# Plain 32-bit products for the first 16 slots of a fused attention and MLP kernel, with a lead of one slot and a new order of the lead-in

## The chip, the cores and the metric

The kernel runs on one core of one Trainium2 chip. The metric is the device time of one launch in microseconds, as the median of several runs.

## What is computed

Batch 8, 8 heads, 576 tokens, head dimension 64; 32 packed queries per head. Attention goes in two steps, then come two MLPs one behind the other, on 4608 tokens:

```python
p_packed = sm_attn(p, k, v)
out = sm_attn(q, p_packed, p_packed)
x = out.transpose(0, 2, 1, 3).reshape(4608, 512)
h = np.maximum(x @ w_in, 0.0)
x = h * h @ w_out
h = x @ w_in2
return (h * (1.0 / (1.0 + np.exp(-1.702 * h)))) @ w_out2
```

The four weights arrive as 64-bit floats and are turned into 32-bit ones on the chip. `w_in` and `w_in2` are 512 x 2048, the other two 2048 x 512.

## The kernel before, in words

**Slots.** The first MLP is cut into slots, one for each (batch b, half hf of 288 tokens, block fc of 128 hidden units). `runs` (L645) lists their order: slots 0 to 3 are (0, 0, fc 0 to 3), 4 to 11 are (0, 1, fc 0 to 7), 12 to 15 are (0, 0, fc 4 to 7), 16 to 31 are the two halves of batch 1 with fc 0 to 7, 32 to 63 are fc 8 to 15 of both batches. From slot 64 on each half takes its 16 blocks in one go. The attention's last product is folded into the MLP: `m_step` (L363) multiplies the packed values by `w_in` into M, and `mm1` (L377) multiplies M by the attention weights `a`. `mm1` is followed by a ReLU and a square on ScalarE, `gsplit` (L393) splits the result, and `mm2` (L397) multiplies by `w_out` into four PSUM banks. In mm1 two inner blocks, in mm2 four output blocks make the products of a slot.

**Split products.** An operand is split into a rounded high part (a copy on ScalarE into the type fp32r) and the rest (a subtraction on VectorE); a product is then three matmuls of fp32r, high by high, high by low, low by high (`prod`, L80). mm1 is 6 and mm2 12 matmuls of 288 columns. The products of the attention itself, `heads` (L247), are plain 32-bit floats; in the trace each of them is two instructions.

**Lead.** The loop at L888 emits, for slot s, `gsplit` of slot s + LA - 1, `mm1` of slot s + LA and `mm2` of slot s, with LA = 3, and then the steps planned for slot s. Each engine runs its instructions in the order in which they are emitted. Steps that are generators are interleaved with each other at their yields (`interleave`, L687).

**Conversions.** A weight block of 128 x 512 is loaded raw (`raw_load`, four buffers), turned into two 32-bit parts on ScalarE (`conv_a`, L113) and joined in three instructions on VectorE (`conv_b`, L122). A block of `w_out` is then split as well (`wo_item`, L143). The list `cq` (L657) is their order; a step `convert` does part b of one item, part a of the next, and `ahead` then issues the raw load of a later one on SP, which waits until a raw buffer is free. `win_item` (L201) also stores pairs of converted blocks of `w_in` to DRAM (`win_d`), from where the later batches load them.

**Lead-in.** Slots -10 to -1 hold the attention of batch 0: `s1` (scores), `s1b` (exponentials), `tr` (transposes), `pv`, `t2`, then `s2a`, `s2b`, `s2c` for each half of the queries, `m_step`, and transposes of the identity called `warm` (L697). The table `first` (L713) is written by hand and also holds the steps of batch 1's attention and the conversions up to slot 35. The loads of batch 1 stand at L764 to L787: keys and values in slot -4, queries in slots 0 to 4, `w_in` from slot 5 on. SP issues all transfers from one queue, in order.

**Rest.** From slot 256 on the second MLP runs in another scheme (L806 on), which the change does not touch.

Of the kernel before, what the change touches and what calls it, by code (L numbers as in the profile page):

```python
# [44 lines left out]
def fused_kernel(ctx, tc, qT, kT, vv, pT, w_in, w_out, w_in2, w_out2, out):  # L45
# [155 lines left out]
    def win_item(f, c):  # L201
        g = c // 2

        def dst():
# [4 lines left out]
        def done(x):
            if c % 2:  # L210
                nc.sync.dma_start(out=win_d[:, f, 2 * g:2 * g + 2, :], in_=wt[0, f, g])

        return conv_item(f"win{f}_{c}", w_in[c * P:(c + 1) * P, f * 512:(f + 1) * 512], dst, done)
# [183 lines left out]
    def mm2(b, hf, fc, seg):  # L397

        t = gh.pop((b, hf, fc))
        w = wo1[fc // 4]  # L400

        ops = [(d, w_, 0) for d in range(NDM) for w_ in (0, 1)] + [(d, 0, 1) for d in range(NDM)]
        for d, w_, x_ in ops:
            if fc == seg[0] and (w_, x_) == (0, 0):
# [522 lines left out]
```

## Time and profile before

| | |
|---|---|
| three runs | 1450.52, 1443.46, 1443.74 us; median 1443.74 |
| the profiled execution | 1446.43 us |
| its span in the profile | 1444.6 us |
| TensorE busy (page, part 1) | 1417.5 us, 98% |
| VectorE, ScalarE busy | 955.2 us (66%), 837.3 us (58%) |
| mean granted clock | 0.993 |

A span is shown from its own start. PE is TensorE, DVE VectorE, ACT ScalarE, SPq the queue of SyncE that issues transfers; a row of a timeline is start, length, engine, line, operation, written tile <- read tiles, count, and in brackets the idle time before it with what ended it.

### The profile page before, as it was taken

Reading aid. Unit: us, or ns where it says so; the run is one execution under the profiler, and the core shown is the slowest. Engines: PE = TensorE matmul, PEld = TensorE weight load, DVE = VectorE, ACT = ScalarE, POOL = GpSimd, SP = SyncE. Lnnn points to the kernel's source line nnn. Section 1 sums busy time; section 2 is a strip of 40 time slices with the busy share of each in tenths; the row PEclk is TensorE's granted clock in tenths of the full one; section 3 lists DMA queues with packets and bytes.
Section 4 is the critical chain, followed back from the end, with each engine's and each line's share of the span. In section 5 each row is a group of like instructions: output and inputs, shape, how many; then the busy total and the mean of one; then the engine's idle time right before and its main releaser. Section 6 shows DMA issues by size and latency. Waiting matters only on the chain.

```text
span 1444.6 us, 24988 instructions
## 1 busy us (share of the span) xinstructions
PE 1417.5 (98%) x9786; PEld 1268.4 (88%) x9786; DVE 955.2 (66%) x1633; ACT 837.3 (58%) x1748; POOL 0.7 (0%) x6
## 2 busy tenths in 40 slices
PE   6799999999999999999999999999999999999999
PEld 4679989989999898999998888888888889999998
DVE  5787476665757748563255778568756876677585
ACT  3888667667676767766564544455444634544452
POOL 0000000000000000000000000000000000000000
PEclk8899999999999999999999999999999999999999
DMA  8756657586574765642145567656765676688675
GB/s 303 241 191 217 227 179 251 164 260 204 184 238 152 257 207 182 201 155 77 50 159 173 205 226 251 217 183 245 252 218 184 217 250 235 251 305 290 253 294 179
DMA packets 110934, 307.95 MB, mean 213 GB/s; under 512 B 9056, under 2 KB 52192, under 8 KB 96736
## 3 DMA queue, kind: packets, MB, share of 16 engines
q1 hardware_dynamic: 110816, 306.35, 61.9%
q8 instruction: 77, 1.26, 0.4%
q14 instruction: 41, 0.34, 0.1%
HBM read 250.94 MB, written 55.38 MB: 212 GB/s over the span
## 4 chain that ended last, share of the span: by engine, by line
PE 90%; DMA 3%; DVE 3%; ACT 3%; issue 1%; SPq 0%; ACTq 0%; DVEq 0%
PE h L86 36%; PE y L406 25%; PE o L86 24%; PE m L255 2%; DMA w_d<-wc 1%; PE s L255 1%; PE pv L313 1%; PE tr_a L301 1%; DMA wA<-w_d 1%; DMA win<-win_d 0%; DMA k<-in_kT 0%; ACT M L370 0%; ACT gh L77 0%; ACT r L385 0%; ACT gf L390 0%
## 5 line engine op out<-in xcount | busy, mean ns | idle before, releaser
L406 PE MATMUL y<-gh,wo 128*128 128x288 f32 x3072 | 449.6, 295 | 3.3 <-ACT ysb L419 2.5
L406 PEld LDWEIGHTS y<-gh,wo 128*128 128x128 f32 x3072 | 421.0, 189 | 4.7 <-ACT ysb L419 3.5
L86 PE MATMUL h<-y,wA 128*128 128x512 f32 (+1 forms) x1680 | 349.5, 367 | 0.2 <-DMA wA<-w_d 0.2
L86 PE MATMUL o<-g,wB 128*128 128x512 f32 (+1 forms) x1680 | 348.9, 367 | 0.0
L86 PEld LDWEIGHTS h<-y,wA 128*128 128x128 f32 x1680 | 305.6, 188 | 40.6 <-issue 0.5
L86 PEld LDWEIGHTS o<-g,wB 128*128 128x128 f32 x1680 | 305.7, 188 | 39.3 <-DMA wB<-w_d 0.2
L86 PE MATMUL h<-a,M 128*128 128x288 f32 x1536 | 257.6, 303 | 8.4 <-ACT a L359 3.0
L86 PEld LDWEIGHTS h<-a,M 128*128 128x128 f32 x1536 | 217.7, 190 | 52.7 <-issue 29.1
L517 ACT ACTIVATE g<-hid 128x1024 fp32r<-128x1024 f32 (+1 forms) x140 | 132.8, 971 | 131.9 <-DVE hid L512 105.3
L78 DVE TENSOR_TENSOR gh<-gf,gh 128x288 fp32r<-128x288 f32 x256 | 115.6, 453 | 123.7 <-ACT gh L77 123.4
L493 DVE TENSOR_TENSOR g<-hid,g 128x1024 fp32r<-128x1024 f32 (+1 forms) x140 | 152.7, 1115 | 42.5 <-ACT g L517 41.2
L385 ACT ACTIVATE r<-h 128x288 f32<-128x288 f32 x256 | 104.0, 406 | 86.5 <-PE h L86 85.9
L581 ACT ACTIVATE r<-h 128x512 f32<-128x512 f32 (+1 forms) x120 | 66.5, 554 | 117.1 <-PE h L86 115.0
L589 DVE TENSOR_TENSOR hid<-h,r 128x512 f32<-128x512 f32 (+1 forms) x120 | 76.2, 635 | 80.2 <-PE h L86 64.3
L77 ACT ACTIVATE gh<-gf 128x288 fp32r<-128x288 f32 x256 | 112.0, 438 | 4.5 <-DVE gf L388 2.7
L599 DVE TENSOR_TENSOR hid<-hid,sg 128x512 f32<-128x512 f32 (+1 forms) x120 | 76.0, 634 | 47.2 <-ACT sg L595 47.2
L390 ACT ACTIVATE gf<-r 128x288 f32<-128x288 f32 x220 | 97.9, 445 | 7.0
L595 ACT ACTIVATE sg<-hid 128x512 f32<-128x512 f32 (+1 forms) x120 | 70.2, 585 | 30.6 <-DVE hid L589 30.3
L372 DVE TENSOR_TENSOR M<-m,M 128x512 fp32r<-128x512 f32 x64 | 43.3, 689 | 46.0 <-ACT M L370 45.2
L512 DVE TENSOR_TENSOR hid<-hid 128x1024 f32<-128x1024 f32 (+1 forms) x60 | 66.1, 1112 | 0.0
L370 ACT ACTIVATE M<-m 128x512 fp32r<-128x512 f32 x64 | 37.1, 595 | 43.6 <-PE m L255 43.5
L255 PE MATMUL m<-win,ppT 64*32 64x512 f32 x512 | 37.7, 615 | 5.8 <-DVE s2t L334 5.0
(93 smaller groups left out, 916.7 us busy)
## 6 DMA issues: line engine op xcount, KB each, us to landing
wB<-w_d SPq DMA_DIRECT2D x70, 1024.0 KB, 4.9
wA<-w_d SPq DMA_DIRECT2D x40, 1024.0 KB, 4.9
wA<-w_d SPq DMA_DIRECT2D x40, 768.0 KB, 6.1
win<-win_d SPq DMA_DIRECT2D x56, 512.0 KB, 5.3
w_d<-wc SPq DMA_DIRECT2D x112, 256.0 KB, 4.0
k<-in_kT SPq DMA_DIRECT2D x32, 288.0 KB, 5.4
y_d<-ysb SPq DMA_DIRECT2D x16, 576.0 KB, 3.8
v<-in_vv SPq DMA_DIRECT2D x16, 512.0 KB, 6.9
```

Source lines behind the costliest of these rows:

```text
L77: nc.scalar.activation(hi, src, AF.Copy)
L78: nc.vector.tensor_tensor(out=lo, in0=src, in1=hi.bitcast(F32), op=ALU.subtract)
L86: nc.tensor.matmul(ps, w, x, start=start and i == 0, stop=stop and i == n - 1, skip_group_check=more)
L255: nc.tensor.matmul(ps[r][32 * hp:32 * hp + 32, :n], w(hp)[rows], xx, start=True, stop=True)
L385: nc.scalar.activation(r, ps[:, :HS], AF.Relu)
L390: nc.scalar.activation(g, r, AF.Square)
L406: nc.tensor.matmul(accs[d][:, :HS], w[:, fc % 4, w_, d * P:(d + 1) * P], t[:, x_, :], start=fc == seg[0] and (w_, x_) == (0, 0), stop=fc = ...
L493: nc.vector.tensor_tensor(out=t[:, :, 1, :n], in0=src, in1=t[:, :, 0, :n].bitcast(F32), op=ALU.subtract)
L517: nc.scalar.activation(t[:, :, 0, :PAIRS[p]], gop[p, i, g, "src"], AF.Copy)
L589: nc.vector.tensor_tensor(out=hid(p, c, blk), in0=bank[p, c, b][:, :n], in1=part[p, c, r][:, 0, :n], op=ALU.add)
L595: nc.scalar.activation(t, bank[p, c, "1"][:, :n] if blk == 2 else hid(p, c, blk), AF.Sigmoid, scale=GELU)
L599: nc.vector.tensor_tensor(out=hid(p, c, blk), in0=bank[p, c, "1"][:, :n] if blk == 2 else hid(p, c, blk), in1=part.pop((p, c, "sg", blk)), ...
```

## The change

The products of the slots of batch 0 with fc below 8 (16 slots, NFULL = 8) are made in plain 32-bit floats, without splits: `mm1` is two products, `mm2` four. M for these blocks is copied by ScalarE alone; M and `a` share a tile (`mf_tile`), the converted blocks 0 to 7 of `w_out` lie unsplit in one tile. The splits of those blocks (`wo_split`) and of `a` (`a_split`) are made later, in slots 10 to 19, 23 and 28, for the slots that use them. The lead is one slot up to slot 7, two up to slot 10 and three after. Slots -10 to -2 become one list, `lead_in`, in which each step is run to its end before the next (`drain`). Conversions 0 to 15 are steps `ca` and `cb` with fixed places; the list `cq` has another order; the stores of `w_in` become steps of their own (`win_store`); batch 1's loads move to slots 0, 1 and 3 to 7. Some steps use other PSUM banks, and for batch 0 the copies of `tr` change engines.

```diff
+NFULL = 8
+NDIR = 16
...
+        def dst():
+            if fc == 0:
+                wo1["f"] = wo_p.tile([P, NFULL, DM], F32, tag="wo", name="wof")
+            return wo1["f"][:, fc]
+
         def use(x):
-            if fc % 4 == 0:
-                wo1[fc // 4] = wo_p.tile([P, 4, 2, DM], F32R, tag="wo", name=f"wo{fc // 4}")
-            w = wo1[fc // 4][:, fc % 4]
-            nc.scalar.activation(w[:, 0, :], x, AF.Copy)
-            yield
-            nc.vector.tensor_tensor(out=w[:, 1, :], in0=x, in1=w[:, 0, :].bitcast(F32), op=ALU.subtract)
-
-        return conv_item(f"wo{fc}", w_out[fc * P:(fc + 1) * P, :], use=use)
+            return wo_split(fc, x)
+
+        return conv_item(f"wo{fc}", w_out[fc * P:(fc + 1) * P, :], *((dst,) if fc < NFULL else (None,)),
+                         use=no_use if fc < NFULL else use)
+
+    def wo_split(fc, x=None):
+        if fc % 4 == 0:
+            wo1[fc // 4] = wo_p.tile([P, 4, 2, DM], F32R, tag="wo", name=f"wo{fc // 4}")
+        w = wo1[fc // 4][:, fc % 4]
+        return late_split(w[:, 0, :], w[:, 1, :], wo1["f"][:, fc] if x is None else x)
+
+    def late_split(hi, lo, x):
+
+        nc.scalar.activation(hi, x, AF.Copy)
+        yield
+        nc.vector.tensor_tensor(out=lo, in0=x, in1=hi.bitcast(F32), op=ALU.subtract)
...
+    def win_store(f):
+        for g in range(2):
+            nc.sync.dma_start(out=win_d[:, f, 2 * g:2 * g + 2, :], in_=wt[0, f, g])
...
+        ta_ = t[:, 0:4, :].rearrange("p c k -> p (c k)")
+        if b == 0:
+            nc.vector.tensor_copy(ta_, pa_)
+            nc.scalar.activation(t[:64, 4, :], pb_[:64, :P], AF.Copy)
+        else:
+            nc.scalar.activation(ta_, pa_, AF.Copy)
+            nc.vector.tensor_copy(t[:64, 4, :], pb_[:64, :P])
...
+    def s2p(b, hf):
...
+    def a_split(hf):
+        a = a_tile(0, hf)
+        return late_split(a[:, :, 0, :], a[:, :, 1, :], mf_tile(hf)[:, 1024:1024 + S].rearrange("p (u n) -> p u n", u=2))
...
+        if b == 0 and 4 * f < NFULL:
+            for r in range(2):
+                nc.scalar.activation(mf_tile(f)[:, 512 * r:512 * r + 512], ps[r], AF.Copy)
+            return
...
+        if full(b, fc):
+            for g in range(2):
...
+                nc.tensor.matmul(ps[:, :HS], w, mf_tile(hf)[:, 1024 + g * HS:1024 + (g + 1) * HS], start=g == 0, stop=g == 1)
...
+            t = gh[b, hf, fc] = gh_p.tile([P, 2, HS], F32, tag="gh", name=f"gh_{b}_{hf}_{fc}")
+            nc.scalar.activation(t[:, 0, :], r, AF.Square)
...
+            ops = [(d, 0, wo1["f"][:, fc]) for d in range(NDM)]
...
+    for w in ((0, 0), (0, 1), (0, 2), (0, 3), range(0, 4), (1, 0), (1, 1), (1, 2), (1, 3), range(4, 12), (2, 0), (2, 1), (2, 2), (2, 3),
+              (3, 0), (3, 1), (3, 2), (3, 3), range(12, 16)):
...
+    for f, *a in ((load_p, 0), (load_k, 0, 0), (load_k, 0, 1), (load_k, 0, 2), (load_k, 0, 3), (ahead,), (ahead,),
+                  (load_v, 0, 0), (load_v, 0, 1), (ahead,), (load_q, 0, 0, 0), (load_q, 0, 1, 0),
+                  (load_q, 0, 2, 0), (load_q, 0, 3, 0), (ahead,)):
         at(S0, f, *a)
 
+    lead_in = [(s1, 0, 0), (s1, 0, 1), (warm, 14), (ca, 0), (s1b, 0), (cb, 0), (tr, 0, 0), (ca, 1), (tr, 0, 1), (cb, 1),
+               (warm, 8), (ca, 2), (pv, 0, 0), (pv, 0, 1), (warm, 2), (t2, 0), (load_q, 0, 0, 1), (load_q, 0, 1, 1),
+               (load_q, 0, 2, 1), (load_q, 0, 3, 1), (cb, 2), (ca, 3), (s2p, 0, 0), (warm, 24),
+               (s2a, 0, 0), (ca, 4), (cb, 3), (win_store, 0), (m_step, 0, 0), (s2b, 0, 0), (ca, 5), (s2p, 0, 1), (warm, 6)]
+    for f, *a in lead_in:
+        at(S0, drain, f, *a)
+    nconv = 6
...
-        -10: [(warm, 14), (s1, 0, 0), (s1, 0, 1)],
...
+        -1: [(cb, 4)],
+        0: [(cb, 5), (ca, 6)],
+        1: [(s2a, 0, 1), (cb, 6), (ca, 7)],
+        2: [(s2b, 0, 1), (cb, 7), (ca, 8), (s1, 1, 0)],
+        3: [(s1, 1, 1), (cb, 8), (ca, 9), (cb, 9), (ca, 10)],
+        4: [(cb, 10), (s1b, 1), (ca, 11), (cb, 11)],
+        5: [(win_store, 1), (m_step, 0, 1), (ca, 12), (cb, 12)],
+        6: [(tr, 1, 0), (ca, 13), (cb, 13), (ca, 14)],
+        7: [(pv, 1, 0), (tr, 1, 1), (cb, 14), (ca, 15)],
+        8: [(pv, 1, 1), (t2, 1), (cb, 15)],
+        9: [(s2a, 1, 0)],
+        10: [(s2b, 1, 0), (wo_split, 0), (wo_split, 1)],
+        11: [(s2c, 1, 0), (m_step, 1, 0), (convert,)],
+        12: [(wo_split, 2), (convert,)],
+        13: [(wo_split, 3), (convert,)],
+        14: [(s2a, 1, 1)],
         15: [(m_step, 1, 1)],
-        16: [(convert,)],
-        17: [(convert,)],
-        18: [(s2b, 1, 1)],
-        19: [(s2c, 1, 1), (convert,)],
-        21: [(m_step, 0, 2)],
-        23: [(convert,)],
-        24: [(convert,)],
+        16: [(wo_split, 4), (convert,)],
+        17: [(wo_split, 5), (convert,)],
+        18: [(s2b, 1, 1), (wo_split, 6)],
+        19: [(s2c, 1, 1), (wo_split, 7)],
...
+        23: [(a_split, 0), (convert,)],
+        24: [(win_store, 2), (m_step, 0, 2), (convert,)],
...
+        28: [(a_split, 1), (convert,)],
...
-            at_k, at_v, at_q, at_w = -4, -4, (0, 2, 3, 4), 5
+            at_k, at_v, at_q, at_w = 0, 1, (3, 5, 6, 7), 7
...
+    nsplit = nfirst = 0
     for s in range(S0, len(slots)):
-        if 0 <= s + LA - 1 < len(slots):
-            slots[s + LA - 1][1](*slots[s + LA - 1][3])
-        if 0 <= s + LA < len(slots):
-            slots[s + LA][0](*slots[s + LA][3])
+        la = LA if s > 10 else 2 if s > 7 else 1
+        while nsplit < min(s + la, len(slots)):
+            slots[nsplit][1](*slots[nsplit][3])
+            nsplit += 1
+        while nfirst < min(s + la + 1, len(slots)):
+            slots[nfirst][0](*slots[nfirst][3])
+            nfirst += 1
```

## Rows read from the trace of the kernel before

**Rows 1.** The page, part 4: the chain that ended last, by engine.
```profile
PE 90%; DMA 3%; DVE 3%; ACT 3%; issue 1%; SPq 0%; ACTq 0%; DVEq 0%
```

**Rows 2.** Busy time by stretch: us, each engine (instructions), PEclk, DMA share, GB/s.
```profile
0.00:107.77 107.77, 85.93 (x765) 66.25 (x766) 79.12 (x164) 74.49 (x166) 0.70 (x6) 0.90 0.72 245
103.00:143.00 40.00, 39.31 (x319) 36.34 (x318) 33.12 (x65) 33.48 (x77) 0.00 (x0) 1.00 0.61 203
```

**Rows 3.** Timeline of TensorE, 0 to 175 us.
```profile
18.83 2.95 PE L702 MATMUL warm<-ident 128*128 128x128 f32 x14
...
23.16 1.75 PE L702 MATMUL warm<-ident 128*128 128x128 f32 x14
...
46.30 0.46 PE L86 MATMUL h<-a,M 128*128 128x288 f32 x1 [2.96 <-ACT a L359]
...
72.49 0.90 PE L313 MATMUL pv<-v,e1t 128*32 128x64 f32 x40
73.32 0.66 PE L301 MATMUL tr_a<-ident,e 128*128 128x128 f32 x4
...
80.34 0.71 PE L255 MATMUL s<-q,ppT 64*32 64x288 f32 x16
...
107.77 0.95 PE L86 MATMUL h<-a,M 128*128 128x288 f32 x6
108.55 1.75 PE L406 MATMUL y<-gh,wo 128*128 128x288 f32 x12
110.14 0.95 PE L86 MATMUL h<-a,M 128*128 128x288 f32 x6
...
119.72 1.09 PE L255 MATMUL m<-win,ppT 64*32 64x512 f32 x16
```

**Rows 4.** Groups by form on TensorE: count, busy us, mean ns, idle before.
```profile
L255 PE MATMUL m<-win,ppT 64*32 64x512 f32 x512 | 37.7, 615 | 5.8 <-DVE s2t L334 5.0 <-DMA win<-win_d 0.8
L255 PE MATMUL s<-k,p 64*32 64x288 f32 x256 | 13.8, 421 | 1.8 <-DMA k<-in_kT 1.2 <-ACT e L269 0.6
```

**Rows 5.** The chain in order of time, 0 to 140 us: start, length, what.
```profile
10.61 2.04 ACT e L284 x8
...
13.21 0.57 ACT r_win L120
```

**Rows 6.** Timeline of VectorE, 0 to 62 us.
```profile
13.49 0.41 DVE L124 TENSOR_SCALAR win<-win 128x512 int32<-128x512 int32 x1
...
14.77 0.69 DVE L128 SCALAR_TENSOR_TENSOR win<-raw_win,win 128x512 int32<-128x512 int32 x1
...
19.01 0.48 DVE L334 STREAM_TRANSPOSE s2t<-s 128x288 f32<-128x288 f32 x1 [0.95 <-PE s L255]
...
23.55 0.75 DVE L336 TENSOR_REDUCE s2st<-s2t 128x18 f32<-128x576 f32 x1
...
28.40 0.78 DVE L354 STREAM_TRANSPOSE s2x<-s2t 128x576 f32<-128x576 f32 x1
```

**Rows 7.** Timeline of ScalarE, 0 to 62 us.
```profile
25.60 0.68 ACT L343 ACTIVATE s2t<-s2t 128x576 f32<-128x576 f32 x1 [1.62 <-DVE s2t L338]
...
32.93 1.08 ACT L370 ACTIVATE M<-m 128x512 fp32r<-128x512 f32 x2 [3.04 <-PE m L255]
...
37.60 0.61 ACT L148 ACTIVATE wo<-x_wo 128x512 fp32r<-128x512 f32 x1
```

**Rows 8.** Busy time by stretch of 2 us, columns as in rows 2.
```profile
20.00:22.00 2.00, 2.00 (x10) 1.56 (x9) 0.96 (x3) 1.25 (x2) 0.00 (x0) 0.50 1.02 414
24.00:26.00 2.00, 0.91 (x9) 0.67 (x7) 1.56 (x3) 0.40 (x1) 0.00 (x0) 1.00 0.16 66
46.00:48.00 2.00, 1.37 (x5) 1.10 (x6) 1.93 (x4) 2.00 (x5) 0.00 (x0) 0.62 0.35 139
48.00:50.00 2.00, 2.00 (x10) 2.00 (x10) 1.97 (x6) 1.97 (x5) 0.00 (x0) 0.52 0.01 2
```

**Rows 9.** The page, part 6: transfers: count, KB each, us from issue to landing.
```profile
k<-in_kT SPq DMA_DIRECT2D x32, 288.0 KB, 5.4
```

More of the change, by code (lines that the diff above doesn't have):

```diff
@@ L207, in dst @@
             return wt[0, f, g][:, c % 2, :]
[L209 to L213, printed above, removed]
+        return conv_item(f"win{f}_{c}", w_in[c * P:(c + 1) * P, f * 512:(f + 1) * 512], dst)
+    def win_store(f):
+        for g in range(2):
+            nc.sync.dma_start(out=win_d[:, f, 2 * g:2 * g + 2, :], in_=wt[0, f, g])
     kt, qt, vt, pt, wt = {}, {}, {}, {}, {}
@@ L326, in fused_kernel @@
     NB = HS // 32
+    def s2p(b, hf):
+        ps = s2t[b, hf] = [att_tile(b, hf == 0, f"s2_{b}_{hf}_{r}") for r in range(2)]
+        heads(ps, lambda hp: ppT[b][:, 32 * hp:32 * hp + 32], lambda hp: qt[b, hp][:, hf * HS:(hf + 1) * HS])
     def s2a(b, hf):
-        ps = [att_tile(b, False, f"s2_{b}_{hf}_{r}") for r in range(2)]
-        heads(ps, lambda hp: ppT[b][:, 32 * hp:32 * hp + 32], lambda hp: qt[b, hp][:, hf * HS:(hf + 1) * HS])
+        if (b, hf) not in s2t:
+            s2p(b, hf)
+        ps = s2t[b, hf]
         t = s2_p.tile([P, 2 * NB, 32], F32, tag="s2t", name=f"s2t{b}_{hf}", bufs=1)
@@ L375, in fused_kernel, with full @@
     gf, gh, ys = {}, {}, {}
+    def full(b, fc):
+        return b == 0 and fc < NFULL
     def mm1(b, hf, fc, seg):
@@ L399, in mm2 @@
         t = gh.pop((b, hf, fc))
[L400 to L404, printed above, removed]
+        if full(b, fc):
+            ops = [(d, 0, wo1["f"][:, fc]) for d in range(NDM)]
+        else:
+            w = wo1[fc // 4][:, fc % 4]
+            ops = [(d, 0, w[:, i]) for d in range(NDM) for i in (0, 1)] + [(d, 1, w[:, 0]) for d in range(NDM)]
+        for n, (d, x_, w) in enumerate(ops):
+            first = fc == seg[0] and d not in {o[0] for o in ops[:n]}
+            if first:
                 accs[d] = acc_p.tile([P, 512], F32, tag=f"acc{d}", name=f"y_{b}_{hf}_{d}_{fc}")
-            nc.tensor.matmul(accs[d][:, :HS], w[:, fc % 4, w_, d * P:(d + 1) * P], t[:, x_, :],
-                             start=fc == seg[0] and (w_, x_) == (0, 0), stop=fc == seg[1] and x_ == 1)
+            nc.tensor.matmul(accs[d][:, :HS], w[:, d * P:(d + 1) * P], t[:, x_, :],
+                             start=first, stop=fc == seg[1] and d not in {o[0] for o in ops[n + 1:]})
         if fc == seg[0] > 0:
@@ L654, in at @@
         plan[s].append((f, a))
[L657 to L660 removed]
+    cq = []
+    for w in ((0, 0), (0, 1), (0, 2), (0, 3), range(0, 4), (1, 0), (1, 1), (1, 2), (1, 3), range(4, 12), (2, 0), (2, 1), (2, 2), (2, 3),
+              (3, 0), (3, 1), (3, 2), (3, 3), range(12, 16)):
+        cq += [win_item(*w)] if isinstance(w, tuple) else [wo_item(fc) for fc in w]
     cq += [None, None]
@@ L681, in convert @@
             at(s, conv_a, a)
-        if b:
+        if b and n > NDIR:
             at(s, conv_b, b)
-        if 0 <= n - 1 < len(cq):
+        if 0 <= n - 1 < len(cq) and n > NDIR:
             plan_end[s] += 1
@@ L755, in fused_kernel @@
     }
+    nconv = NDIR
     for s, steps in first.items():
```

85 lines of the change are left out of this document (42 added, 43 removed).

## The prediction

> **What bounds the kernel now.** I read the views from the outside in. The chain that ended last is TensorE for 90% of the span [rows 1], so only two things can count: the TensorE work itself, and the stretches in which TensorE waits or runs at its lower clock. A table by stretch tells where those are [rows 2]: up to 107.77 us TensorE is busy for 85.9 us at a mean granted clock of 0.90; from 103 to 143 us it is busy for 39.3 of 40 us at 1.00, while VectorE has 33.1 and ScalarE 33.5. So the change is worth what it does before about 108 us, and may cost something where a filled VectorE and ScalarE get more work. The row at 107.77 [rows 3] is my marker: there the 17th mm2 has ended and 20 mm1 are done. The new program has done the same products at that point of its order, so the difference of the marker, and of what follows, is the difference of the run. The profiled execution took 1446.43 us (span 1444.6), 2.7 us over the median of 1443.74. I work out a difference in the profile and take it off the median.
>
> **Term 1, price of a plain product.** mm1 of 6 instructions takes 0.78 us (107.77 to 108.55) and mm2 of 12 takes 1.59 us (to 110.14) [rows 3]: 0.132 us for an instruction of 288 columns. No plain product of 128 by 128 is in the trace. The nearest rows are the small plain ones of L255, two instructions to a product: a group of 16 takes 1.09 us with 512 columns and 0.71 us with 288 [rows 3], and a single instruction 615 and 421 ns on the mean [rows 4]. The latter is 0.87 ns for a column, 2.08 cycles at 2.4 GHz. So I take twice the streaming time: 288 columns are 0.120 us at one cycle, 0.240 at two, and the 0.012 of overhead stays: 0.253 us. Ends: 0.132 (as cheap as a split one) and 0.264 (twice all of it). A plain mm1 is 4 instructions, 1.01 us; mm2 is 8, 2.02 us; the slot 3.03 instead of 2.37. On 16 slots TensorE gets 10.6 us **more** work. This can pay only if waits go.
>
> **Term 2, lead-in to the first mm1.** Its start is unchanged: the four exponentials run from 10.61 for 2.04 us [rows 5]. The two conversion instructions on ScalarE that now stand ahead of them (0.57 us [rows 5] each) fit before 10.61 if the first raw weights are there; I take 0, at most 0.8. From 12.7 VectorE carries the chain. A conversion, drained in one piece, is 13.49 to 14.77 plus 0.69, 1.9 us [rows 6]. In order (small steps are put at 0.2 to 0.3 each): sums 0.4, conversion 0, two 128x512 copies of the transposes, which are new on VectorE (no row; between 0.48, the transpose of 288 columns [rows 6], and 0.75, the reduction of 576; I take 0.65 each), conversion 1, two scalings: 18.8. Transpose and copy of ppT 0.6: 19.4; the score group at the lower clock 1.4: 20.8, by when conversion 2 is done. Two transposes at 0.48 and two operations near 0.75 [rows 6], 2.3: 23.1; conversion 3: 25.0; m_step 1.02 to 1.09 [rows 3]: 26.0; its two copies on ScalarE stand ahead of the second exponential, 1.08 [rows 7]: 27.1; s2b, from 25.60 [rows 7] to 28.40 plus 0.78 [rows 6] now, 3.6: **30.7**. The split of the activations and the subtractions of M no longer come before it.
>
> A clock rule bears on the 24 transposes called warm. The row first: while 14 such transposes and a few small products ran from 18.83 us in 2.95 us [rows 3], the granted clock was 0.50 at 20 to 22 us [rows 8]; the next 14, from 23.16, took 1.75 us [rows 3], and 24 to 26 us shows 1.00 [rows 8]. Transposes brought 2.4 GHz back here. The Trainium skill ("TensorE: Matmul & The Clock Gate", Part 4: PE-mode transpose) says that transpose mode does not count as TensorE activity in that way. By that rule the new transposes are wasted, and the first mm1 comes 2.8 us later, as the third rival works out; this trace disagrees, so the sum goes by the rows.
>
> **Term 3, slots 0 to 3.** VectorE converts two wo blocks (30.7 to 34.5), and only then can SP issue the keys of batch 1, moved from slot -4 to 0 behind those raw loads: five issues, some 2 us, landing 5.4 us after [rows 9], about 42. TensorE has 4 mm1 and 3 mm2, 10.1 us, with one stretch at the lower clock: 42.5 or so. The score group and the first maximum come next, 0.7 and 0.4, and they are **ahead of the rest of s2b(0,1) on VectorE**: 2.9 more. mm1 of slot 4 starts at 46.5.
>
> **Term 4, slots 4 to 7.** With a lead of one slot the engines wait in turn. s1(1,1) stands behind mm1(4) and mm2(3): 3.7 us in which VectorE's queue is held by its first maximum. Then two conversions and three small steps, 4.95; then ScalarE's exponentials 2.04, the conversion's two parts 1.13, and what VectorE still has of conversion 11, 1.5. m_step(0,1) at 46.5 + 13.3 = 59.8; TensorE has had 6.1 us of products in 9.6 us. After that it is dense: m_step 1.0, two slots 6.1, two transposes of 0.7 and a pv of 0.83 (72.49 to 73.32) [rows 3], 9.3: slot 7 ends at 69.1.
>
> **Term 5, slots 8 to 16.** 7 plain and 4 split mm1 7.1 + 3.1; 8 plain mm2 and one split 16.2 + 1.6; pv 0.8; t2 0.4; two score groups 1.3; two m_steps 2.0: 32.5. Marker at 101.6. Both long waits (3.1 and 3.5 us) may drop the clock: an idle 2.96 us ahead of 46.30 [rows 3] was followed by 0.62 and 0.52 [rows 8], a loss of 0.76 + 0.96 = 1.7 us. I take one of two: **103.3**, 4.5 us before 107.8.
>
> **Term 6, slots 16 to 31.** The splits of wo 0 to 7 and of two activations move here or just ahead, and the conversions come later: 14 conversions on VectorE instead of 10, 8 more subtractions of wo and 2 of a, taken at 0.69 and 0.75 like other operations of their sizes [rows 6]: 7.6 + 5.5 + 1.5 = 14.6 us on 33.1 of 40 [rows 2], 47.7. On ScalarE 3 more conversions and 10 more copies (0.61 [rows 7]): 3.4 + 6.1 on 33.5, 43.0. Both exceed TensorE's 40. The splits of g run two slots ahead, 4.7 us, and swallow most of VectorE's 7.7; the stretch also begins before the marker, so part of the 33.1 belongs to earlier slots. I take 1.5 lost, ends 0 and 14.6 (VectorE's idle 6.9 us stays as well).
>
> The four win_d stores and batch 1's v and q loads, moved on SP, cost nothing: their readers come slots later, and the raw loads behind them have two conversions of time; without that cover each would show as one landing, 5.4 us [rows 9]. The fifth wo tile in four buffers is first wanted ten slots after its buffer is free: nothing. The 16 splits of g that go save VectorE and ScalarE work but lie beside TensorE.
>
> Sum: -4.5 + 1.5 = -3.0 us: 1443.74 - 3.0 = **1440.7**.
>
> **Rivals.** *The waits of terms 3 and 4 are mostly hidden* (raw data early, conversions interleaved at less than 1.9 us, no drop of the clock). With no wait at all from 30.7 on, the marker is 30.7 + 16 x 3.03 + 4 x 0.78 + 1.59 + 9.1 for batch 1's attention = 93.0, 14.8 us early: the bound. Half of it, and term 6 as forecast: 1434. For: the removed splits are just what VectorE had most of; against: the order written out puts a score group ahead of the s2b. Chance 0.26. *VectorE becomes the bound in slots 16 to 31*, the slower side: its 47.7 us come with most of the waits it has today, TensorE loses 12.5 us and it is 1451.7; it decides once its backlog passes the two slots (4.7 us) by which the splits lead. For: 47.7 against 40; against: the two slots of lead, and the part of the 33.1 that is older work. Chance 0.12. *Transposes do not hold the clock*: 24 of them at 0.21 end at 25.9 instead of 25.0 and m_step takes 2.0 instead of 1.0, so with the group before it everything is 2.8 later: 1443.5; rows 3 and 8 speak against it. Chance 0.08. *The plain product is not dearer* (0.132 us an instruction): slots 8 to 15 alone take 1.4 us less each, 1429; the 2.08 cycles speak against. Chance 0.04.
>
> **The numbers.** The forecast holds 0.50; by itself it lies between 1436 and 1447. Under 0.5% (7.2 us) a measurement of this kernel can hardly tell from no change. Faster: the first rival's and the last one's greater part, 0.29; slower: nearly all of the second, 0.11; same 0.60. The range 1431 to 1450 leaves out the last rival, the first's far end and the second's far half, under 0.2.
>
> **What would show it.** Plain instructions near 253 ns apart in dense slots (9 to 12); the first mm1 at 30 to 32 us; VectorE idle before a maximum of L266 in slots 2 and 3, TensorE idle before m_step(0,1); marker between 101 and 106; single waits of TensorE on L78 or L77 between slots 18 and 31. It is wrong if TensorE is dense from slot 0 on, if the marker is earlier than 99 or later than 108, or if over 4 us of idle time appear after it.

## The result, and the profile after

The changed kernel takes **1456.19 us** (median of 9 runs, 1453.74 to 1460.98) against 1443.9 (9 runs, 1441.68 to 1450.52): ratio 1.0079, 95% interval 1.0060 to 1.0098. It is slower by some 11 us; the forecast was 1440.7, with 1450 as the upper end. The profiled execution took 1456.19 us, with a span of 1454.4.

The chain that ended last, from the page of the changed kernel, answers to [rows 1]: TensorE holds still more of it.

```profile
PE 93%; DMA 2%; DVE 2%; ACT 2%; issue 0%; SPq 0%; DVEq 0%; ACTq 0%
```

Busy time by stretch of the changed kernel, columns as in [rows 2]:

```profile
0.00:106.98 106.98, 88.91 (x656) 59.39 (x657) 64.78 (x128) 59.94 (x133) 0.70 (x6) 0.94 0.71 234
103.00:143.00 40.00, 37.78 (x277) 34.21 (x276) 34.11 (x66) 33.32 (x74) 0.00 (x0) 0.96 0.52 168
107.00:160.00 53.00, 47.22 (x341) 42.44 (x340) 43.92 (x82) 45.11 (x102) 0.00 (x0) 0.90 0.70 228
120.00:122.00 2.00, 2.00 (x10) 2.00 (x10) 1.88 (x4) 2.00 (x5) 0.00 (x0) 0.50 0.01 4
156.00:158.00 2.00, 2.00 (x9) 1.75 (x8) 1.71 (x3) 1.29 (x4) 0.00 (x0) 0.50 1.06 344
```

The same view of the kernel before, for the third of these stretches:

```profile
107.00:160.00 53.00, 53.00 (x437) 49.74 (x437) 38.30 (x76) 43.37 (x104) 0.00 (x0) 1.00 0.75 253
```

Up to the marker the two kernels are nearly level: VectorE has 14 us less work, TensorE 3 us more. From 107 to 160 us TensorE loses nearly 6 us to waits and 10% of its clock, where the kernel before had neither.

The same view between two marks that are the same point of the work in both kernels, the marker and the first scores of batch 2, first before, then after:

```profile
107.77:148.25 40.48, 40.48 (x322) 38.31 (x320) 31.26 (x60) 34.87 (x82) 0.00 (x0) 1.00 0.69 230
106.98:158.03 51.05, 45.27 (x323) 41.40 (x321) 42.69 (x79) 44.35 (x100) 0.00 (x0) 0.92 0.69 225
```

Here VectorE has 11.4 us and ScalarE 9.5 us more work than before. Each of them is now busy for longer than the 40.48 us that TensorE needs for its own work in this stretch, ScalarE by 3.9 us.

The timeline of TensorE of the changed kernel, 20 to 160 us, shows where. The row at 106.98 is the marker of [rows 3]; the one at 158.03 begins the scores of batch 2.

```profile
21.20 2.84 PE L769 MATMUL warm<-ident 128*128 128x128 f32 x24
...
31.75 4.18 PE L437 MATMUL h<-Mf 128*128 128x288 f32 x8 [3.44 <-DVE Mf L383]
35.72 2.83 PE L473 MATMUL y<-gh,wof 128*128 128x288 f32 x8
...
48.66 2.29 PE L437 MATMUL h<-Mf,Mf 128*128 128x288 f32 x4 [3.58 <-DVE Mf L383]
50.74 3.84 PE L473 MATMUL y<-gh,wof 128*128 128x288 f32 x8
...
65.23 1.05 PE L270 MATMUL m<-win,ppT 64*32 64x512 f32 x4 [1.53 <-DVE win L130]
...
74.22 2.11 PE L437 MATMUL h<-Mf 128*128 128x288 f32 x8
...
86.33 2.10 PE L437 MATMUL h<-Mf,Mf 128*128 128x288 f32 x8
88.27 2.10 PE L473 MATMUL y<-gh,wof 128*128 128x288 f32 x8
...
106.98 0.95 PE L88 MATMUL h<-a,M 128*128 128x288 f32 x6
...
118.14 0.40 PE L88 MATMUL h<-a,M 128*128 128x288 f32 x1 [1.51 <-ACT a L402]
118.94 1.45 PE L88 MATMUL h<-a,M 128*128 128x288 f32 x5 [0.39 <-DVE a L404]
...
154.85 3.25 PE L473 MATMUL y<-gh,wo 128*128 128x288 f32 x12 [3.56 <-ACT ysb L486]
...
158.03 1.21 PE L270 MATMUL s<-k,p 64*32 64x288 f32 x16
```

The **balance in three parts**: the marker comes at 106.98 instead of 107.77 (-0.8); from there to the scores of batch 2 it takes 51.05 us instead of 40.48 (107.77 to 148.25), which is +10.6; from there to the end 1296.4 us in both (1454.4 - 158.03, 1444.6 - 148.25). The sum, +9.8, is the difference of the spans. Between these two executions nothing is lost after 160 us.

The late waits have their reasons in ScalarE's queue. Its timeline in the changed kernel:

```profile
117.41 0.68 ACT L402 ACTIVATE a<-s2x 128x576 fp32r<-128x576 f32 x1 [1.78 <-DVE s2x L383]
...
137.38 0.69 ACT L121 ACTIVATE win<-raw_win 128x512 f32<-128x512 f32 x1 [1.55 <-DMA win_d<-win]
...
151.21 0.67 ACT L121 ACTIVATE x_wo<-raw_wo 128x512 f32<-128x512 f32 x1 [0.85 <-DMA raw_wo<-in_w_out]
...
154.41 1.29 ACT L486 ACTIVATE ysb<-y 128x288 f32<-128x288 f32 x4
```

The copies of the y banks, which the next mm2 waits for, stand at 154.41 behind conversions that themselves waited for a store and for a load; apart from the 0.85 us ScalarE has no gap from 137.38 on. The copy of `a` waits for VectorE's second softmax, which had a subtraction of `wo` between its steps (0.68 us at 114.70).

The early waits, in ScalarE's and VectorE's timelines of the changed kernel:

```profile
27.04 1.09 ACT L415 ACTIVATE Mf<-m 128x512 f32<-128x512 f32 x2 [4.24 <-PE m L270]
28.01 0.68 ACT L368 ACTIVATE s2t<-s2t 128x576 f32<-128x576 f32 x1
```
```profile
28.73 0.75 DVE L370 TENSOR_REDUCE s2st<-s2t 128x18 f32<-128x576 f32 x1 [2.82 <-ACT s2t L368]
...
30.82 0.78 DVE L383 STREAM_TRANSPOSE Mf<-s2t 128x576 f32<-128x576 f32 x1
...
45.14 0.46 DVE L281 TENSOR_REDUCE st<-s 128x1 f32<-128x288 f32 x1 [1.43 <-PE s L270]
...
47.83 0.78 DVE L383 STREAM_TRANSPOSE Mf<-s2t 128x576 f32<-128x576 f32 x1
...
55.43 0.46 DVE L281 TENSOR_REDUCE st<-s 128x1 f32<-128x288 f32 x1 [6.82 <-PE s L270]
```

The exponential of the second softmax (28.01) stands behind the copies of M and VectorE waits 2.82 us for it. In half 1 the rest of that softmax stands behind the first maximum of batch 1 (45.14).

### The profile page after: what moved, and what is told of

Read it like the earlier page. It is cut to its first block, busy times and chain, and to the rows that moved or that the text cites. A ratio compares the mean times of both kernels' runs of the same rounds, so it can differ in the third digit from the quotient of the medians.

```text
span 1454.4 us, 24711 instructions
## 1 busy us (share of the span) xinstructions
PE 1426.4 (98%) x9678; PEld 1265.2 (87%) x9678; DVE 951.5 (65%) x1613; ACT 833.0 (57%) x1732; POOL 0.7 (0%) x6
## 3 DMA queue, kind: packets, MB, share of 16 engines
q8 instruction: 76, 1.25, 0.3%
## 4 chain that ended last, share of the span: by engine, by line
PE 93%; DMA 2%; DVE 2%; ACT 2%; issue 0%; SPq 0%; DVEq 0%; ACTq 0%
PE h L88 37%; PE y L473 27%; PE o L88 23%; PE m L270 2%; PE s L270 1%; PE h L437 1%; PE pv L333 1%; DMA wB<-w_d 1%; PE tr_a L316 0%; DMA raw_wo<-in_w_out 0%; DMA win<-win_d 0%; DMA k<-in_kT 0%; DVE win L128 0%; DVE win L130 0%; DMA win_d<-win 0%
## 5 line engine op out<-in xcount | busy, mean ns | idle before, releaser
L473 PE MATMUL y<-gh,wo 128*128 128x288 f32 x2880 | 421.9, 296 | 3.6 <-ACT ysb L486 3.6
L473 PEld LDWEIGHTS y<-gh,wo 128*128 128x128 f32 x2880 | 395.6, 189 | 4.0 <-ACT ysb L486 3.8
L88 PE MATMUL h<-a,M 128*128 128x288 f32 x1440 | 237.6, 300 | 1.9 <-ACT a L402 1.5
L88 PEld LDWEIGHTS h<-a,M 128*128 128x128 f32 x1440 | 202.2, 189 | 39.5 <-issue 28.3
L80 DVE TENSOR_TENSOR gh<-gf,gh 128x288 fp32r<-128x288 f32 x240 | 108.4, 453 | 123.8 <-ACT gh L79 120.9
L79 ACT ACTIVATE gh<-gf 128x288 fp32r<-128x288 f32 x240 | 105.0, 437 | 4.1 <-DVE gf L450 2.3
L452 ACT ACTIVATE gf<-r 128x288 f32<-128x288 f32 x204 | 90.7, 445 | 6.5
L270 PE MATMUL m<-win,ppT 64*32 64x512 f32 x512 | 40.8, 601 | 3.4 <-DVE win L130 2.8
```

The source lines that it names most:

```text
L79: nc.scalar.activation(hi, src, AF.Copy)
L80: nc.vector.tensor_tensor(out=lo, in0=src, in1=hi.bitcast(F32), op=ALU.subtract)
L88: nc.tensor.matmul(ps, w, x, start=start and i == 0, stop=stop and i == n - 1, skip_group_check=more)
L270: nc.tensor.matmul(ps[r][32 * hp:32 * hp + 32, :n], w(hp)[rows], xx, start=True, stop=True)
L452: nc.scalar.activation(g, r, AF.Square)
L473: nc.tensor.matmul(accs[d][:, :HS], w[:, d * P:(d + 1) * P], t[:, x_, :], start=first, stop=fc == seg[1] and d not in {o[0] for o in ops[n ...
```

## The experiments

All edits are to the changed kernel. Two families of theories stand against each other. By the first the loss is made between slots 16 and 32, where ScalarE and VectorE got the late splits, the conversions and their transfers; the waits at `a` and `ysb` go when that work moves. By the second it is made in the lead-in and the first slots, by the dearer products, the short lead and the order of the steps. A letter in an expectation names the theory that is spelled out beside it. The runs in one table, with marks from one profiled execution each (us):

| run | first mm1 | marker | scores of batch 2 | span | median | ratio to before, 95% interval |
|---|---|---|---|---|---|---|
| changed kernel | 31.75 | 106.98 | 158.03 | 1454.4 | 1456.19 | 1.0079 (1.0060 to 1.0098) |
| e1_splits_early | 31.29 | 107.75 | 156.48 | 1454.6 | 1456.85 | 1.0088 (1.0069 to 1.0106) |
| e2_store_at_conversion | 31.73 | 105.97 | 156.62 | 1457.9 | 1458.07 | 1.0092 (1.0077 to 1.0107) |
| e3_both_backlogs | 30.21 | 106.26 | 154.72 | 1451.2 | 1454.58 | 1.0072 (1.0054 to 1.0090) |
| e4_warm_first | 31.87 | 105.94 | 156.44 | 1456.9 | 1455.77 | 1.0081 (1.0066 to 1.0096) |
| e5_spread_and_stores | 30.20 | 105.48 | 148.23 | 1448.9 | 1449.67 | 1.0031 (1.0021 to 1.0041) |
| e6_scores_later | 30.50 | 101.17 | 151.95 | 1451.0 | 1454.38 | 1.0060 (1.0041 to 1.0079) |
| e7_all | 30.54 | 103.00 | 146.51 | 1445.1 | 1446.99 | 1.0015 (1.0003 to 1.0026) |
| e8_half_mm2 | 30.76 | 101.18 | 151.46 | 1451.8 | 1455.25 | 1.0069 (1.0054 to 1.0084) |
| e9_four_plain_blocks | 30.77 | 109.31 | 152.49 | 1449.8 | 1451.45 | 1.0031 (1.0018 to 1.0043) |
| e10_s2b_before_m | 28.51 | 96.00 | 138.79 | 1439.4 | 1441.02 | 0.9958 (0.9945 to 0.9970) |
| e11_both | 27.93 | 100.03 | 143.22 | 1442.6 | 1444.48 | 0.9987 (0.9976 to 0.9998) |
| e12_s2b_alone | 27.22 | 96.07 | 146.74 | 1445.5 | 1448.89 | 1.0019 (1.0009 to 1.0030) |

A span is good to some 2 to 3 us only: after 160 us single waits of TensorE, mostly on loads of weights from DRAM, sum to 0.7 us in the changed kernel's execution and to 1.7 to 5.4 in the experiments'. Effects on the time are read from the ratios. The start differs as well from one execution to another: with the same lead-in (all rows but those of e4, e7 and e9 to e12) the first exponential begins at 10.57 to 12.11 us, as the keys land, and the first mm1 comes at 30.20 to 31.75. The stretch from the marker to the scores of batch 2 is free of that.

### The late splits of wo

```diff
-        8: [(pv, 1, 1), (t2, 1), (cb, 15)],
-        9: [(s2a, 1, 0)],
-        10: [(s2b, 1, 0), (wo_split, 0), (wo_split, 1)],
+        8: [(pv, 1, 1), (t2, 1), (cb, 15), (wo_split, 0), (wo_split, 1), (wo_split, 2)],
+        9: [(s2a, 1, 0), (wo_split, 3), (wo_split, 4)],
+        10: [(s2b, 1, 0)],
...
-        18: [(s2b, 1, 1), (wo_split, 6)],
-        19: [(s2c, 1, 1), (wo_split, 7)],
+        18: [(s2b, 1, 1)],
+        19: [(s2c, 1, 1)],
```

(Splits 5 to 7 go to slots 11 and 12.)

> Only the places of the eight splits of the first wo blocks change: from slots 10 to 19 to slots 8 to 12, where TensorE has 3 us or more a slot. Theory A (VectorE and ScalarE are overfull in slots 16 to 31): s2b of the second half of batch 1 comes earlier, the wait of 1.51 + 0.39 us on L402 and L404 at 118 us and the 1.7 us of lower clock behind it go; 1452 to 1453, some 3.6 us less; the wait on the y copies at 151 to 155 us stays or shrinks by a part. Rival B (the plain products themselves are the price, and the waits only move): no change, 1456, the same idle time elsewhere. Rival C (the w_in stores as steps of their own hold ScalarE): no change either, since these are not touched.

The wait of 1.51 us at `a` is gone, with no fall of the clock behind it; 0.40 is left. But the time did not fall: the wait at `ysb` stayed, 3.53 us, and ScalarE now waited 2.02 us for the store. The time is what rival B expected. The late splits explain the first late wait, not the time.

### The stores of w_in

```diff
+        def done(x):
+            if f > 1 and c % 2:
+                nc.sync.dma_start(out=win_d[:, f, 2 * g:2 * g + 2, :], in_=wt[0, f, g])
...
-        24: [(win_store, 2), (m_step, 0, 2), (convert,)],
+        24: [(m_step, 0, 2), (convert,)],
```

(The store at slot 30 goes in the same way.)

> Only the stores of the last two blocks of w_in go back to the end of their conversion, as in the kernel before. Rival C (ScalarE's wait of 1.55 us on a w_in store at 137 us and 0.85 on a raw block at 151 us make it late for the y copies): 2.4 us less lag on ScalarE, the wait at 151 to 155 us falls from 3.56 to 1.2 us and its clock loss of 2.6 us goes: 1451. Theory A: the wait falls by 2 us at most and the wait at 118 us stays: 1453 to 1456. Rival B: 1456.

ScalarE no longer waits for a store, but for raw blocks: 2.74 us, and TensorE at `ysb` 4.20 (1.2 expected by rival C). One wait took the other's place.

### Splits early, conversions spread

The edit of the first experiment, and four conversions moved:

```diff
-        19: [(s2c, 1, 1)],
+        19: [(s2c, 1, 1), (convert,)],
...
-        27: [(convert,)],
-        30: [(convert,), (win_store, 3), (m_step, 0, 3)],
-        31: [(convert,)],
-        35: [(convert,)],
+        30: [(win_store, 3), (m_step, 0, 3)],
+        33: [(convert,)],
+        34: [(convert,)],
+        36: [(convert,)],
```

> The early splits of e1, and the conversions of the last four wo blocks spread from slots 29 to 32 to slots 29 to 36 (one conversion moved to slot 19). Theory A: both late waits go with their clock losses, 1.9 + 1.7 + 3.56 + 2.6 = 9.8 us: 1446 to 1447. Rival B: 1454 to 1456, idle time of TensorE in slots 16 to 32 stays above 3 us. Rival C: the wait at 118 us goes, that at 151 us stays by half: 1449 to 1452.

The wait at `ysb` fell to 0.95 us, but a new one came. ScalarE's and TensorE's timelines of this run:

```profile
135.12 0.66 ACT L121 ACTIVATE win<-raw_win 128x512 f32<-128x512 f32 x1 [5.22 <-DMA win_d<-win]
```
```profile
137.50 1.70 PE L88 MATMUL h<-a,M 128*128 128x288 f32 x6 [3.85 <-ACT r L443]
```

A conversion that now comes early wants the buffer whose store waits for its fixed place at slot 24, and the ReLU that TensorE needs stands behind it. By the signs of the expectation this run speaks for rival B (1454 to 1456, over 3 us of idle time); only the next one parts the theories.

### Both together

The edits of the second and the third experiment.

> The early splits and spread conversions of e3 together with the stores of e2, so that ScalarE neither has too much to do nor waits for a w_in store (5.2 us at 130 us in e3). Theory A2 (what stops TensorE in slots 16 to 32 is ScalarE being late, by its load and by its waits for transfers together; each alone leaves the other): no wait of TensorE over 1 us between slots 16 and 32, the score group of batch 2 starts at 149 us instead of 158, and the run comes to 1448 to 1450. Rival B (the plain products are the price, waits only move): another wait of 3 to 4 us turns up in slots 16 to 32 and the run stays at 1453 to 1456.

No wait of TensorE over 1 us is left between 107 and 160 us, and its clock is full there, as the table by stretch of this run shows; the second row goes from the marker to the scores of batch 2:

```profile
107.00:160.00 53.00, 51.67 (x419) 47.72 (x418) 43.42 (x85) 47.56 (x112) 0.00 (x0) 1.00 0.81 265
105.48:148.23 42.75, 41.42 (x322) 38.57 (x320) 36.66 (x69) 40.21 (x93) 0.00 (x0) 1.00 0.75 252
```

The stretch between the marks shrinks from 51.05 to 42.75 us (40.48 before the change), ScalarE's work in it by 4.1 us and VectorE's by 6.0. The ratio falls from 1.0079 to 1.0031, with intervals apart. This is theory A2; rival B falls, since the plain products are the same. The whole edit is shown to win this. Early splits alone, stores alone, and early splits with spread conversions each leave a wait of 3.5 to 4.2 us; the spread conversions alone, and each of the other two pieces with the stores, were not run, so which pieces are needed stays open.

### The lead-in: transposes, scores, dearer products

```diff
-    lead_in = [(s1, 0, 0), (s1, 0, 1), (warm, 14), (ca, 0), (s1b, 0), (cb, 0), (tr, 0, 0), (ca, 1), (tr, 0, 1), (cb, 1),
+    lead_in = [(warm, 14), (s1, 0, 0), (s1, 0, 1), (warm, 14), (ca, 0), (s1b, 0), (cb, 0), (tr, 0, 0), (ca, 1), (tr, 0, 1), (cb, 1),
```

> Only 14 transposes are put back ahead of the first score groups, where the kernel before has them. If the score groups ran slow because TensorE came to them cold: the four exponentials start at 10.6 instead of 12.1 us, the first mm1 at 30.3 instead of 31.75, and 1.5 us come off the end: 1454.7. If the keys set that time: exponentials at 11.5 or later and 1456.

The second case holds: the exponentials began at 12.22 us, and the first mm1 came at 31.87. The first scores wait for their keys (1.79 us on that load ahead of 24 products at 7.87 us), warm or not.

```diff
-        2: [(s2b, 0, 1), (cb, 7), (ca, 8), (s1, 1, 0)],
-        3: [(s1, 1, 1), (cb, 8), (ca, 9), (cb, 9), (ca, 10)],
-        4: [(cb, 10), (s1b, 1), (ca, 11), (cb, 11)],
-        5: [(win_store, 1), (m_step, 0, 1), (ca, 12), (cb, 12)],
+        2: [(s2b, 0, 1), (cb, 7), (ca, 8)],
+        3: [(cb, 8), (s1, 1, 0), (ca, 9)],
+        4: [(cb, 9), (s1, 1, 1), (ca, 10), (cb, 10), (ca, 11)],
+        5: [(s1b, 1), (cb, 11), (win_store, 1), (m_step, 0, 1), (ca, 12), (cb, 12)],
```

> Only the two score groups of batch 1 go one slot later, behind the conversions of their slots, so that VectorE's queue is not held by a maximum that waits for TensorE. Theory D (with a lead of one slot the engines wait in turn in slots 2 to 5): VectorE's idle 6.8 us before L281 at 55 us shrinks under 3 us, mm1 of slot 4 starts at 47 instead of 48.7, m_step(0,1) ends at 60 instead of 66.2, and the marker behind the 17th mm2 at 101 instead of 107; the end 4 to 6 us earlier, if the late waits stay as they are, less if VectorE and ScalarE turn out to set slots 16 to 32. Rival E (the conversions set the time of m_step(0,1) anyway): 66 and 107, no change.

The wait at slot 4 fell from 3.58 to 2.51 us, the second m_step of batch 1 came at 97.67 instead of 103.49, and the waits at `a` and `ysb` stayed at 1.49 and 3.24. The marker came at 101.17, as theory D expected, though 1.25 us of this is an earlier start in this execution (first mm1 at 30.50). The end did not follow by 4 to 6 us: the ratio fell by 0.0019, with intervals that overlap.

```diff
-            ops = [(d, 0, wo1["f"][:, fc]) for d in range(NDM)]
+            ops = [(d, 0, wo1["f"][:, fc]) for d in range(NDM if fc in seg else 2)]
```

> Ten of the sixteen plain mm2 (those that neither begin nor end a group) leave out two of their four output blocks, so the output blocks 2 and 3 lack these terms: 40 instructions at 0.2425 us, 9.7 us of TensorE work less, 5.8 of them in the dense slots 7 to 14. If the plain products' time is on the path in slots 7 to 15 and late waits are set from the marker on: marker 6 us earlier and 1449 to 1451. If slots 0 to 15 are set by VectorE's conversions: marker under 2 us earlier. If slots 16 to 32 are set by ScalarE and VectorE in absolute time: marker 6 us earlier, but the late waits grow by about that and the run stays at 1454 to 1456.

With 9.7 us of TensorE's work left out, the scores of batch 2 came 6.6 us earlier and the ratio fell by only 0.0010. The marker came 5.8 us earlier, and the late waits, 1.44 and 3.78 us, did not move. None of the three cases holds as stated: the first has the marker right and the end wrong, the third has the end right, but the late waits did not grow.

### All repairs so far

The edits of e4_warm_first, e5_spread_and_stores and e6_scores_later.

> e5, e6 and the transposes of e4 in one. Theories A2 and D: gains add up, 6 to 7 from the late waits, 5 from the early ones and 1 from the start: 1442 to 1445, about level with the kernel before. Rival B: above 1450. If it comes below 1442 the plain products pay once the waits are gone.

1446.99 us, 0.15% over the kernel before: less than rival B's 1450, but above the 1442 to 1445 that the gains in sum should have given.

### The place of the second softmax, and fewer plain blocks

In the kernel before, `s2b` of half 0 stood a slot ahead of `m_step`; the change turned this round.

```diff
-               (s2a, 0, 0), (ca, 4), (cb, 3), (win_store, 0), (m_step, 0, 0), (s2b, 0, 0), (ca, 5), (s2p, 0, 1), (warm, 6)]
+               (s2a, 0, 0), (ca, 4), (cb, 3), (win_store, 0), (s2b, 0, 0), (m_step, 0, 0), (ca, 5), (s2p, 0, 1), (warm, 6)]
...
-        0: [(cb, 5), (ca, 6)],
-        1: [(s2a, 0, 1), (cb, 6), (ca, 7)],
-        2: [(s2b, 0, 1), (cb, 7), (ca, 8), (s1, 1, 0)],
+        0: [(cb, 5), (ca, 6), (s2a, 0, 1)],
+        1: [(cb, 6), (ca, 7), (s2b, 0, 1)],
+        2: [(cb, 7), (ca, 8), (s1, 1, 0)],
```

So `s2b` goes ahead of `m_step` again, and in half 1 `s2a` and `s2b` each go to the end of the slot before (earlier, where the expectations also say "later"). First on top of e7_all (whose slot 2 has no s1), with a second kernel in which only fc 0 to 3 are plain, and a third with both:

```diff
-NFULL = 8
+NFULL = 4
+NWOF = 8
...
+        6: [(wo_split, 4), (tr, 1, 0), (ca, 13), (cb, 13), (ca, 14)],
+        7: [(wo_split, 5), (pv, 1, 0), (tr, 1, 1), (cb, 14), (ca, 15)],
+        8: [(wo_split, 6), (pv, 1, 1), (t2, 1), (cb, 15)],
+        9: [(s2a, 1, 0), (wo_split, 7), (a_split, 0)],
```

(`a_split` of half 1 goes to slot 5, the `wo` splits 0 to 3 to slots 11 to 14; NWOF is the number of unsplit blocks kept.)

> All earlier repairs (e7_all), and in the lead-in the second softmax of half 0 goes ahead of the four M copies, the second softmax of half 1 one step earlier and later in slots 0 to 2. Theory D (the start and the first waits are set by the order in ScalarE's queue: the exponential stands behind M's copies): first first-layer product at 28 to 29.5 instead of 30.5, the waits of slots 0 to 4 shrink by 1 to 3 us in sum, score group of batch 2 at 142 to 145, 1442 to 1445 us. Rival (VectorE's chain of the second softmax and the half clock behind a wait set them): first product at 30 or later, waits of slots 0 to 4 within 1 us of e7_all's, 1446 to 1448 us.

> All earlier repairs together (the run e7_all), and only the first 8 slots (d_ff blocks 0 to 3) in plain floats: blocks 4 to 7 get their split weights and their split attention output by slot 9, so 8 slots go back from 2.91 us to 2.37. Theory P (the plain products' price is paid in full once no wait hides it): 8 x 0.54 = 4.3 us less than e7_all, score group of batch 2 at 142 to 144 instead of 146.5, about 1442.7 us, ratio 0.997 to 1.0. Theory Q (the splits that come back, 8 of weights, 2 of the attention output and 8 of the gelu output before slot 16, load ScalarE and VectorE where batch 1's prologue needs them): new TensorE waits of 3 us or more in slots 5 to 16, score group of batch 2 not before 146, 1446 us or more.

> e9_four_plain_blocks and e10_s2b_before_m together. If both hold, the gains add: score group of batch 2 at 138 to 141, 1438 to 1441 us, faster than the kernel before by 0.2 to 0.4 per cent. If theory Q or the rival of e10 holds, 1444 us or more, level with the kernel before.

**e10_s2b_before_m takes 1441.02 us** (1438.04 to 1441.98), ratio 0.9958: faster than both kernels, and than the 1442 to 1445 expected. The first mm1 starts at 28.51 with a wait of 0.53 us, and the wait at slot 4 shrinks from 2.51 (in e7) to 0.74; the timeline of TensorE of this run:

```profile
28.51 2.18 PE L441 MATMUL h<-Mf 128*128 128x288 f32 x8 [0.53 <-ACT wof L121]
...
39.47 1.24 PE L441 MATMUL h<-Mf,Mf 128*128 128x288 f32 x4 [0.74 <-DVE Mf L387]
```

Fewer plain blocks cost time: by the ratios 0.0029 in e11 against e10 (intervals apart) and 0.0016 in e9 against e7 (intervals overlap), although TensorE has 8 x 0.54 = 4.3 us less to do. The cost lies ahead of the marker, which comes 4.0 and 6.3 us later; from there to the scores of batch 2 e9 and e11 take 43.2 us, e7 and e10 43.5 and 42.8. TensorE's timeline of e11_both:

```profile
58.60 0.66 PE L321 MATMUL tr_a<-ident,e 128*128 128x128 f32 x4 [1.59 <-DVE M L427]
...
75.55 1.57 PE L89 MATMUL h<-a,M 128*128 128x288 f32 x5 [1.93 <-DVE a L168]
```

It waits for VectorE's subtractions of M and of `a`, and with the short lead for the two parts of a split of g (0.44 and 0.41 us). That is the mechanism of theory Q, though no single wait reaches the 3 us that it named; the largest wait hangs on where I put `a_split`, so another placement of four plain blocks stays open.

Then the new place by itself, on the changed kernel:

> The changed kernel with the second softmax's new place alone (ahead of the four M copies in the lead-in, half 1 a step later in the slots), none of the repairs of the backlogs. If the waits of the later slots take back what is won early (as in e6_scores_later and e8_half_mm2): first first-layer product at 28 to 29.5 instead of 31.75, wait at slot 4 under 1.5 us instead of 3.58, the first row of batch 1's first scores at 39 to 42 instead of 44.3, the waits at a and ysb in slots 16 to 32 still 4 to 6 us in sum, 1451 to 1454 us. If the early gain passes through to the end: 1449 us or less, 7 us under the changed kernel's 1456.

The second case holds for the time, which is just inside its 1449 us; the waits named in the first case came too, without taking the gain back. The exponential and the end of the softmax, in ScalarE's and VectorE's timelines of this run:

```profile
23.01 0.67 ACT L368 ACTIVATE s2t<-s2t 128x576 f32<-128x576 f32 x1
25.43 1.09 ACT L415 ACTIVATE Mf<-m 128x512 f32<-128x512 f32 x2 [1.74 <-PE m L270]
```
```profile
26.29 0.78 DVE L383 STREAM_TRANSPOSE Mf<-s2t 128x576 f32<-128x576 f32 x1
```

and TensorE's:

```profile
27.22 2.18 PE L437 MATMUL h<-Mf 128*128 128x288 f32 x8 [0.53 <-DVE Mf L383]
...
40.49 1.24 PE L437 MATMUL h<-Mf,Mf 128*128 128x288 f32 x4
...
107.24 0.40 PE L88 MATMUL h<-a,M 128*128 128x288 f32 x1 [1.52 <-ACT a L402]
...
143.56 3.25 PE L473 MATMUL y<-gh,wo 128*128 128x288 f32 x12 [3.17 <-ACT ysb L486]
```

The end of the transpose moves from 31.60 to 27.07. Of these 4.5 us 1.6 are an earlier start in this execution (first exponential at 10.52 instead of 12.11); 2.9 are the edit's, the shorter wait ahead of the first mm1 (0.53 instead of 3.44). The wait at slot 4 is gone, and from 20 to 40 and from 40 to 60 us the granted clock is 1.00 where the changed kernel had 0.83 in both. The marker comes at 96.07 instead of 106.98. The ratio falls by 0.0060, 8.7 us, with intervals apart, though both late waits are nearly as long as before. So there are **two independent losses** of nearly one size: the place of the second softmax is worth 0.0060 here and 0.0057 on top of e7, the backlogs between slots 16 and 32 are worth 0.0048. The marks part them too: the marker is at 96.0 to 96.1 in both e10 and e12, and from it to the scores of batch 2 it takes 42.8 to 43.5 us in e5, e7 and e10, but 50.3 to 51.1 in the changed kernel, e2, e4, e6, e8 and e12. With the small edits of e4 and e6, e10 has won 0.0121. What half 0's order and half 1's earlier softmax win each was not run apart, nor was the new order with split products only: whether the plain products pay by themselves stays open.

## Why the prediction was wrong

- **Term 1, the price of a plain product: the mechanism right, the size 4% high.** From 86.33 to 88.27 eight instructions of 288 columns take 1.94 us, 0.2425 each against 0.253. A slot is 12 x 0.2425 = 2.91 us, 0.54 more than before, 8.7 us on 16 slots against 10.6. 0.2425 us for 288 columns are 2.02 cycles to a column at 2.4 GHz, in each of two instructions. This agrees with the four passes that the Trainium skill gives for true FP32 ("FP8 and Floating Point Precision", TensorE Precision Notes). The rival of equal price fell.
- **Term 2, the first mm1: 31.75 instead of 30.7.** The start was not "unchanged": the exponentials begin at 12.11 instead of 10.61 [rows 5]; runs with the same lead-in show 10.57 to 12.11, so this is the keys' landing in this execution. From there to the first mm1 it takes 19.6 us (20.1 in my sum), the exponential behind M's copies included (28.01, forecast 27.1 as the end of the copies). What the order costs stood in my working as steps of the sum: behind conversion 3 come the m_step, the two copies and the exponential, some 2.8 us. e12 shows 2.9, and that it was avoidable I had not weighed. The 24 transposes at 21.20 took 2.84 us at a granted clock of 1.00, and it had been 1.00 through five microseconds of transposes alone (10.68 to 15.65): the rival by which transposes do not hold the clock fell again. In this trace nothing bears out the Trainium skill ("TensorE: Matmul & The Clock Gate", Part 4: PE-mode transpose) where it says that transpose mode does not count as TensorE activity, though here the clock was at its higher level before these transposes began.
- **Terms 3 and 4: the right waits, too low a price.** The first wait, 3.44 us ahead of the first mm1, lies inside term 2. The 6.82 us of VectorE ahead of its maximum at 55.43, the wait at slot 4 and the one at m_step (1.53) are all there; mm1 of slot 4 starts at 48.66 (46.5), slot 7 ends at 74.22 (69.1). I took one fall of the clock at 1.7; there were two, with 3.44 and 3.58 us of waiting. The eight instructions each at 31.75 and 35.72 took 4.18 and 2.83 us instead of 2.1, 2.8 us more in sum; mm1 of slot 4 and the mm2 behind it took 5.9 instead of 2.9, 3.0 us more.
- **Term 5 was right in sum:** 74.22 to 106.98 is 32.8 us (32.5), with products 1.0 us cheaper than taken and the rest 1.3 dearer. The marker missed by the sum of terms 2 to 4: 106.98 against 103.3, a gain of 0.8 instead of 4.5.
- **Term 6 is the step that failed:** 1.5 us taken, 10.6 lost. Its upper end, 14.6, held it, and the second rival (12.5 lost, chance 0.12) has nearly its size, but not its mechanism: it has VectorE alone as the bound. The surplus of work that the term worked out was there: ScalarE is busy for 44.35 us between the marks (43.0 forecast) and VectorE for 42.69 (47.7), against 40.48 of TensorE. What failed is the cover: I let the two slots by which the splits of g run ahead swallow VectorE's surplus, and gave ScalarE's 3 us no price at all. The lead did cover the splits of g, where no wait of TensorE over 0.3 us is left. TensorE stopped elsewhere, at `a` and at `ysb`, whose copies stand in ScalarE's queue behind late conversions and behind VectorE's late softmax, neither of which the lead covers. "The four win_d stores ... cost nothing" is a part of that failure: 1.55 us of ScalarE here, 5.22 in e3. e5, which moves splits, conversions and stores, shows that they make up most of the loss together (51.05 to 42.75 us). Behind both waits the clock fell to 0.50. The sign that the prediction named, over 4 us of idle time behind the marker, is what came.

The waits in sum explain only part of the 10.6: 1.51 + 0.39 + 0.31 + 3.56 = 5.8 us. The products that ran at the low clock, from 118.94 to 122.83 and from 154.85 to 158.03, took some 3.2 us more than the same products before the change. Another 1.0 is the m_step at 130.04, which a wait cuts in two: without the wait it takes 2.06 us instead of 1.02, at a granted clock of 1.00. The remaining 0.6 lies in the ends of the rows beside the waits.

One sum of the prediction is off: half of the first rival's 14.8 us, with term 6 as forecast, gives 1437.8 and not 1434. That is within the 0.5% (7.2 us) that the prediction counts as the same, so the 0.29 for "faster" was too high by its own measure.

What stays open: e6 and e8 brought the scores of batch 2 forward by 6.1 and 6.6 us, but the time fell by 2.7 and 1.4 by the ratios, with intervals that overlap the changed kernel's. In their executions TensorE waits 2.8 and 3.9 us after 160 us instead of 0.7; an earlier start does not explain them, since e2 and e4, whose scores come only 1.4 and 1.6 us earlier, have 4.9 and 4.7 us of such waits. Where these gains went is not shown.

## What to carry to other kernels

A step that is moved out of the lead-in lands in front of somebody else: read in each engine's queue which release for TensorE stands behind it. Sums of busy time between two marks of the same work tell that an engine is overfull (ScalarE 44.4 us against TensorE's 40.5), but not where TensorE will stop; a lead covers only the releases that it moves ahead. An exponential that a chain waits for goes ahead of copies that nothing waits for yet; that order, with half 1's softmax a step earlier, was worth 0.6% here. Pieces of work that share a buffer, a store and a load are best tried as a group: here a piece moved alone, or two of them, only exchanged one wait for another.
